# Attention into a squared-ReLU feed-forward: another order for the early columns of L1, weight sets stored from another queue, and earlier norms for two pairs of heads

## The chip, the cores and the metric

The kernel runs on one core of a Trainium2 chip. Its engines have an instruction queue each and run in order: TensorE (PE, matrix products), VectorE (DVE), ScalarE (ACT), GpSimd (POOL) and SyncE (SP, which here only issues DMAs). A queue goes on when the semaphores that its next instruction waits for have come. The metric is the time of one execution on the device in microseconds, as the median of some runs; a profile of one further execution shows each instruction.

## The reference

Two blocks follow one another, in float32; the two weight matrices come as float64.

```python
# q, k, v: (8, 12, 448, 64)
def rmsnorm(x, g):
    rms = np.sqrt(np.mean(x * x, axis=-1, keepdims=True) + 1e-06)
    return x / rms * g
q_n, k_n = (rmsnorm(q, g_q), rmsnorm(k, g_k))
scores = scale * np.matmul(q_n, k_n.transpose(0, 1, 3, 2))
scores = scores - np.max(scores, axis=-1, keepdims=True)
attn = np.exp(scores)
attn = attn / (np.sum(attn, axis=-1, keepdims=True) + 1e-09)
attn_out = np.matmul(attn, v).astype(np.float32)

x = np.ascontiguousarray(attn_out.transpose(0, 2, 1, 3)).reshape(B * S, H * D)   # (3584, 768)
h = x @ w_in            # (3584, 2048)
r = np.maximum(h, 0.0)
g = r * r
return (g @ w_out).astype(np.float32)   # (3584, 768)
```

## The kernel before

**Spans and pairs.** The eight batches are worked on in four spans of two. The twelve heads are taken as six pairs, so a span has twelve pairs of heads: pairs 0 to 11 are span 0, pairs 12 to 23 span 1, and so on. Both large products, L1 (`x @ w_in`) and L2 (`g @ w_out`), are done in the Strassen-Winograd manner: the weights and the activations are split into quadrants, and seven products stand for eight. Of the weights the seven blocks are called A11, S2, S1, S3, A12, A22, S4. The activations' sums are held in `xC` (for L1) and `gC` (for L2) beside `xT` and `gT`, the transposed activations; `combine_x` builds `xC` and `combine` builds `gC`.

**The weights** are prepared once, in span 0, and lie in DRAM as `w1s` and `w2s`. This goes in sets, `n` = 0 to 31 (0 to 15 for `w_in`, 16 to 31 for `w_out`; an even and an odd set make one of 16 groups of seven blocks). The generator `prepare(t)` is a software pipeline cut into four quarters per tick t; `weights(upto)` draws quarters from it until so many have been taken. Counted from the start of tick 0, in tick t stand:

- first quarter: a store of the finished sets (L599, from SP), and DVE clamps the exponents of set t (L604)
- second quarter: ACT converts the low words (L607), DVE shifts bits (L609)
- third quarter: DVE joins the words (L614); POOL makes the totals S3 and S4 of sets t-2 and t-3 (L584), and half a value of set t-1 (L576 on POOL, or, for sets from `MID // 4` on, both halves at once by DVE, L580)
- fourth quarter: ACT takes exponents of set t+1 (L590), POOL the other half value of set t-1 and the totals S1 and S2 (L584), SP loads the words of a later set (L541, L544)

The sets lie in two buffers by turns (`blocks_of`), so a store has to have landed before the second set of blocks after it is written. Three numbers say how far the preparation has come: `EARLY` = 48 quarters by the end of the first stage, `MID` = 86 by the end of the second, `ALL` = 140 in the third.

**The stages of span 0.** They follow one another in program order; the profile's places are in brackets.

1. `attention_alone` (to about 122 us): pairs 0 to 9 (`NAT` = 10), with keys and queries laid out as [112, 4 x ...] per head. Each pair i takes four steps; `norm(i+2)` squares and sums (ACT, DVE), `roots(i+2)` takes the inverse root as Ln and Exp on ACT and one step of refinement on DVE (L730 to L732) and multiplies on POOL (L733). For pairs 10 and 11 the layout is another (`by_squares`: squares of 32 x 32), and `norm(i+2)` at the end of step i calls `squares` (ACT, L740) and `norm_by_squares`: DVE sums, copies and adds (L747 to L752), POOL takes the power -1/2 (L753) and multiplies (L755).
2. The early product with pairs 10 and 11 beside it (122 to 197 us). `first_product(work, 0, 0)` does the blocks A11, S1 and A12 of the first `NE` = 6 of the `HF` = 8 column groups f, three groups of matmuls each, 18 in all (line L1060). `attention(10, 12)` is drawn beside it in 16 pieces, with 38 quarters of the preparation. In it the softmax sums of a pair go out from DVE as `square`, by POOL DMA L1022 to DRAM (`factors`), and come back spread over partitions (L833) into `xT`; DVE multiplies (`finish`, L903), and `combine_x` builds `xC` (L913 to L918, on DVE for pair 11, on POOL for pair 10).
3. `first_product(work, 0)` (197 to 305 us): for f < 6 (`kept`) the other blocks in the order S2, S3, A22, S4, for f = 6 and 7 all seven, 38 groups in all (line L1094). S2 goes into the PSUM tile `pb`, S3 into `pd`, A22 is added onto `pd` once DVE has added `pd` to y and written `g22` (L1112), S4 goes into `pc`. `pb`, `pc` and `pd` take turns in two banks (`bank`, by the counter `turn`). 54 quarters of the preparation are drawn beside it in the first 34 of its 38 steps, and the norms of pairs 12 and 13 (`ahead`).

Then `second_product` of span 0 follows with the attention of span 1 beside it, and so on for the other spans.

**Loads of weight blocks.** `load_blocks(upto)` asks for blocks from `w1s` and `w2s` in the order of their use (`first_uses`, `uses2`), five ahead, into the tile `sw` with five buffers; each is a DMA from SP's queue (L668). It asks only for blocks of sets that count as stored (`written`). SP's queue also carries the loads of q, k and v, the words of the weights, the stores of the sets and the output.

Of the kernel before, what the change touches and what calls it, by code (L numbers as in the profile page):

```python
# [10 lines left out]
F32 = mybir.dt.float32  # L11
U32 = mybir.dt.uint32
AF = mybir.ActivationFunctionType
ALU = mybir.AluOpType
# [373 lines left out]
def attention_then_ffn_bounded(  # L388
# [98 lines left out]
    HW = HC * P  # L487
    WORDS, BLOCKS, EXPS = 7, 2, 4

    EARLY, MID, ALL = 48, 86, 4 * (2 * NFC + 3)  # L490
    assert DM == NW and BLOCKS * 8 * HW + EXPS * NW + 2 * NW <= 3 * HF * S and 2 * NW <= 4 * S and HF % 4 == 0


# [28 lines left out]
    def place_of(n, k):  # L522

        return 7 * int(n >= NFC) if k == A21 else k + int(n < NFC)
# [27 lines left out]
    def prepare(t):  # L552

        def there(n):
            return 0 <= n < 2 * NFC

        def parts(n):
            low, high = pairs_of(words_of(n))  # L560
            return exponents_of(n), exponents_of(n).bitcast(U32), low, high

        def value(n, half):
            if not there(n):
                return

            to = ((A11, A12), (A21, A22)) if n < NFC else ((A11, A21), (A12, A22))
            places = [place_of(n, k) for k in to[n % 2]]
            part = slice(half * HW, (half + 1) * HW)
            if not doubles:  # L570
                nc.gpsimd.tensor_copy(blocks_of(n)[:, places[half]], words_of(n).bitcast(F32)[:, part])
                return
            _, eu, low, _ = parts(n)
            if n < MID // 4:
                dst = blocks_of(n)[:, places[half]]
                nc.gpsimd.tensor_tensor(*[x.bitcast(I32) for x in (dst, low[:, part], eu[:, part])], ALU.add)  # L576
            elif half == 0:
                dst = blocks_of(n)[:, places[0]:places[1] + 1:places[1] - places[0]]
                low, eu = (x.rearrange("p (h m) -> p h m", h=2) for x in (low, eu))
                nc.vector.tensor_tensor(*[x.bitcast(I32) for x in (dst, low, eu)], ALU.add)  # L580

        def total(n, dst, x, y, op):
            if there(n) and n % 2:
                nc.gpsimd.tensor_tensor(*[blocks_of(n)[:, place_of(n, i)] for i in (dst, x, y)], op)  # L584

        def unsigned(n):

            if there(n) and doubles:
                e, _, _, high = parts(n)
                nc.scalar.activation(e, high.bitcast(F32), AF.Abs)  # L590

        if t == 0:
            unsigned(0)
        n = t - 3
        if there(n) and n % 2:
            c = n % NFC // 2
            dst = w1s[c] if n < NFC else w2s[c // 4, :, c % 4]
            first = place_of(n, A11)
            nc.sync.dma_start(dst, blocks_of(n)[:, first:first + 7])  # L599
            written[0] = n + 1  # L600
        if there(t) and doubles:
            e, eu, low, high = parts(t)

            nc.vector.tensor_scalar(e, e, 2.0 ** -15, 1.875 * 2.0 ** 16, ALU.max, ALU.min)  # L604
        yield
        if there(t) and doubles:
            nc.scalar.activation(low.bitcast(I32), low, AF.Copy, scale=2.0 ** -29)  # L607
            bits = banks.get("bits", eu)
            nc.vector.tensor_scalar(bits, eu, 3, 0x3FFFFFF8, ALU.logical_shift_left, ALU.bitwise_and)  # L609
        if t < 3:  # L610
            load_words(t, t - 1)
        yield
        if there(t) and doubles:
            nc.vector.scalar_tensor_tensor(eu, high, 0xC0000000, bits, ALU.bitwise_and, ALU.bitwise_or)  # L614
        total(t - 2, S3, A11, A21, ALU.subtract)
        total(t - 2, S4, A12, S2, ALU.subtract)
        value(t - 1, 0)
        yield
        unsigned(t + 1)
        value(t - 1, 1)  # L620
        total(t - 1, S1, A21, A22, ALU.add)
        total(t - 1, S2, S1, A11, ALU.subtract)
        load_words(t, t - 1)
        yield
# [18 lines left out]
    uses2 = [(m, i) for m in range(HC) for i in (A11, A12)]  # L643
    uses2 += [(m, i) for m in range(HC) for i in (S2, S1, S3, A22, S4)]
    first_uses = [(f, i) for f in range(NE) for i in (A11, S1, A12)]
    first_uses += [(f, i) for f in range(NE) for i in (S2, S3, A22, S4)]
    first_uses += [(f, i) for f in range(NE, HF) for i in range(7)]

    N1 = HF * 7
# [71 lines left out]
    def roots(i):  # L721


        raw, sq = (places_of(qk, i, n)[:SP] for n in range(2))
        rstd = rstds[i]
        flat = rstd.rearrange("p s n -> p (s n)")
        y, t = (small.tile([P, 2 * S // 32], F32, tag=tag, name=tag)[:SP, 0:4 * NJ] for tag in ("half", "other"))
        nc.scalar.activation(y, flat, AF.Ln, scale=2.0 ** -63)
        nc.scalar.activation(y, y, AF.Exp, scale=-0.5, bias=sums["rebias"])
        nc.vector.scalar_tensor_tensor(t, y, -0.5, flat, ALU.mult, ALU.mult)  # L730
        nc.vector.tensor_tensor(t, t, y, ALU.mult)
        nc.vector.scalar_tensor_tensor(flat, t, 1.5, y, ALU.add, ALU.mult)  # L732
        nc.gpsimd.tensor_tensor(sq[:, 0].rearrange("p (j h d) -> p h j d", j=NJ, h=2),  # L733
                                raw[:, 0].rearrange("p (h j d) -> p h j d", j=NJ, h=2),
                                rstd[:, 0].rearrange("p (h j) -> p h j ()", h=2).to_broadcast([SP, 2, NJ, D]),
                                ALU.mult)
# [2 lines left out]
        raw, qkn = (by_squares(i, n).rearrange("p s g e -> p (s g e)") for n in range(2))  # L739
        nc.scalar.activation(qkn, raw, AF.Square)  # L740

    def norm_by_squares(i):
        raw, qkn = (by_squares(i, n) for n in range(2))
        NG = S // 32
        half = small.tile([P, 2 * NG], F32, tag="half", name="half")
        other = small.tile([P, 2 * NG], F32, tag="other", name="other")
        nc.vector.tensor_reduce(half, qkn.rearrange("p s g e -> p (s g) e"), AX, ALU.add)  # L747
        for n in range(4):
            m = n ^ 1
            nc.vector.tensor_copy(other[n * 32:(n + 1) * 32], half[m * 32:(m + 1) * 32])  # L750
        nc.vector.tensor_tensor(half, half, other, ALU.add)
        nc.vector.tensor_scalar(half, half, 1.0 / D, 1e-6, ALU.mult, ALU.add)  # L752
        nc.gpsimd.tensor_tensor(half, half, mhalf, ALU.pow)  # L753
        for s in range(2):
            nc.gpsimd.tensor_tensor(  # L755
                qkn[:, s], raw[:, s],
                half[:, s * NG:(s + 1) * NG].rearrange("p g -> p g ()").to_broadcast([P, NG, 32]), ALU.mult)
        normed[i] = qkn
# [161 lines left out]
    def attention_alone():  # L920


        for i in range(NAT):
            more = i + 1 < NAT
            if 0 < i < NAT - 3:
                load(i + 3)
            scores(i, 0)
            scores(i, 1)
            if i == 0:

                transpose(1, 1, 1)
                scores(0, 2)
                scores(0, 3)
                transpose(1, 0, 0)
                add_up(0, 1)
                norm(2)
                load_v(1)
                values(0, (0, 1))
                load(3)
                yield  # L940
                continue
            if more:
                transpose(i + 1, 1, 0)
            values(i - 1, (2, 3))
            add_up(i, 1)
            if i + 2 < NAT:
                norm(i + 2)
            elif not more:
                load(NAT + 2)
            yield  # L950
            if more:
                transpose(i + 1, 0, 0)
            load_v(i + 1)
            yield
            scores(i, 2)
            scores(i, 3)
            if i + 2 < NAT:
                roots(i + 2)
            total_of(i - 1)
            values(i, (0, 1))  # L960
            finish(i - 1)
            yield
            if added(i) == 3:
                add_up(i, 2)
            combine_x(i - 1)
            if NAT <= i + 3 < NAT + 2:
                load(i + 3)
            if i + 2 >= NAT:
                norm(i + 2)
            yield  # L970
        transposes(NAT)
        values(i, (2, 3))
        total_of(i)
        finish(i)
        combine_x(i)
        if NAT + 2 < 2 * NPAIR:
            squares(NAT + 2)
# [62 lines left out]
    def first_product(work, span, part=1):  # L1040
# [27 lines left out]

        for f in range(HF):
            kept = span == 0 and f < NE  # L1070
            order = (S2, S3, A22, S4) if kept else range(7)
            n = span * (N1 + N2) + f * 7
            if span == 0:
                n = 3 * NE + 4 * f if kept else 7 * f
# [130 lines left out]
    with tc.tile_pool(name="words", bufs=2) as spare["pool"]:  # L1205
# [5 lines left out]
        with tc.tile_pool(name="first", bufs=2, reuse_waits="tile") as work:  # L1211
# [4 lines left out]
            sums["turned"], sums["factors"] = (g[:, 0:S] for g in free[2 * NJ + 2:2 * NJ + 4])  # L1216
            sums["ones"] = work.tile([SP, D], F32, tag="ones", name="ones", bufs=1)
            nc.vector.memset(sums["ones"], 1.0)
            sums["rebias"] = work.tile([SP, 1], F32, tag="rebias", name="rebias", bufs=1)
            nc.vector.memset(sums["rebias"], -31.5 * math.log(2.0))  # L1220
            for u, _ in enumerate(attention_alone()):

# [133 lines left out]
```

## Time and profile before

| | |
|---|---|
| median of 3 runs | 1407.07 us (1401.82 to 1408.52) |
| profiled execution: its time, its span | 1403.64 us, 1401.8 us |
| PE busy | 1344.4 us (96%) |
| DVE, ACT, POOL busy | 851.8, 431.4, 608.1 us |
| SP's queue waiting at L599 for POOL's L584, 0 to 310 us | 52.0 us in 9 waits |
| w1s<-gC and w2s<-gC (stores of sets) | 8 and 8, 1344 KB each, 7.2 and 5.8 us to landing |
| sw<-w1s | 224, 192 KB each, 2.3 us to landing |
| L753, the power of a norm on POOL | 38, 4848 ns each |

How to read it. One execution was profiled. An engine counts as busy while it computes; PE's matmuls are pipelined. The row of slices gives the busy share of 40 equal slices in tenths. A waiting line reads: engine, line, tile that waits <- engine, tile and line that came last, then us in total, number of waits, longest. A line of the timeline reads: start, duration, engine, line, operation, written tile <- read tile, count, and in brackets how long the engine stood idle before and what ended that. "SPq" and "DMA" in it are SP's queue and a transfer. `sw`, `pa` to `pd`, `gT`, `gC`, `xT`, `xC` are the program's tiles; `gC` serves as the staging room of the weights as long as span 0 prepares them.

### The profile page before, as it was taken

The numbers are of one execution on the slowest core, as the hardware profiler recorded it, in microseconds if no ns is written. First come the engines' busy times: TensorE is split into PE (matmuls) and PEld (weight loads), VectorE is DVE, ScalarE is ACT, GpSimd is POOL, SyncE is SP. The second block draws the span as 40 slices with busy tenths as digits, with TensorE's granted clock in tenths as the row PEclk, the third lists the DMA queues.
The fourth block names the chain that finished last, engine by engine and source line by source line (L and its number), as shares of the span: only waits on it lengthen the run. The fifth ranks groups of instructions, "written<-read, shape, count | busy, mean of one in ns | idle before, by whom it ended". The sixth has DMA issues, their size and how long they took to land.

```text
span 1401.8 us, 17013 instructions
## 1 busy us (share of the span) xinstructions
PE 1344.4 (96%) x5646; PEld 641.7 (46%) x5646; DVE 851.8 (61%) x1494; ACT 431.4 (31%) x668; POOL 608.1 (43%) x488
## 2 busy tenths in 40 slices
PE   8997868899999999999999999999999999999998
PEld 3332334444444455544444455554444445555554
DVE  6999857839998633447878723447788743332111
ACT  8884435543333211224333211223333201110000
POOL 6778763526566312445656412355665412221000
PEclk9999999999999999999999999999999999999999
DMA  9786777655667543345566533345656433334443
GB/s 256 209 249 164 272 256 265 182 177 116 126 128 144 120 99 90 85 113 127 125 131 131 128 100 84 90 104 116 133 124 135 107 98 90 85 89 107 106 110 71
DMA packets 428836, 190.66 MB, mean 136 GB/s; under 512 B 290756, under 2 KB 423428, under 8 KB 426692
## 3 DMA queue, kind: packets, MB, share of 16 engines
q1 hardware_dynamic: 421860, 180.39, 50.6%
q0 software_dynamic: 4992, 8.86, 2.4%
q8 instruction: 47, 0.77, 0.2%
q10 hardware_dynamic: 1888, 0.23, 0.1%
q14 instruction: 49, 0.40, 0.1%
HBM read 156.24 MB, written 33.17 MB: 135 GB/s over the span
## 4 chain that ended last, share of the span: by engine, by line
PE 82%; DVE 9%; POOL 3%; DMA 3%; issue 2%; ACT 1%; SPq 0%; POOLq 0%; DVEq 0%; ACTq 0%
PE ps L1163 36%; PE pd L1094 9%; PE pc L1094 9%; PE pa L1094 8%; PE sc L788 7%; PE pav L865 7%; PE pb L1094 4%; DVE gC L614 1%; POOL gC L584 1%; DVE gT L813 1%; DMA sw<-w1s 1%; DMA factors<-square 1%; DVE gC L604 1%; PE sc L796 1%; DVE gC L580 1%
## 5 line engine op out<-in xcount | busy, mean ns | idle before, releaser
L1163 PE MATMUL ps<-gT,sw 128*128 128x448 f32 x752 | 293.0, 543 | 0.0
L1163 PE MATMUL ps<-gC,sw 128*128 128x448 f32 x576 | 225.2, 543 | 0.0
L753 POOL TENSOR_TENSOR half<-half,mhalf 128x28 f32<-128x28 f32 x38 | 184.2, 4848 | 94.5 <-DVE half L752 88.0
L1050 POOL TENSOR_TENSOR gT<-gT 128x448 f32<-128x448 f32 x96 | 94.4, 985 | 289.1 <-ACT gT L1046 289.1
L1163 PEld LDWEIGHTS ps<-gT,sw 128*128 128x128 f32 x752 | 141.2, 190 | 146.3 <-issue 141.6
L1163 PEld LDWEIGHTS ps<-gC,sw 128*128 128x128 f32 x576 | 108.2, 190 | 112.8 <-issue 109.5
L1046 ACT ACTIVATE gT<-gT 128x448 f32<-128x448 f32 x96 | 55.3, 576 | 321.1 <-DVE gT L1112 321.1
L1094 PE MATMUL pa<-xT,sw 128*128 128x448 f32 x312 | 125.8, 540 | 0.0
L788 PE MATMUL sc<-qkT 64*64 64x448 f32 (+1 forms) x1216 | 117.5, 502 | 7.2 <-ACT qkT L765 7.2
L790 ACT ACTIVATE pr<-sc 128x896 f32<-128x896 f32 x89 | 79.3, 915 | 117.9 <-PE sc L788 117.9
L1094 PE MATMUL pb<-xC,sw 128*128 128x448 f32 x192 | 81.1, 561 | 11.9 <-DMA sw<-w1s 10.9
L1094 PE MATMUL pd<-xC,sw 128*128 128x448 f32 x192 | 79.7, 552 | 10.4 <-DVE gT L1112 10.4
L584 POOL TENSOR_TENSOR gC<-gC 128x384 f32<-128x384 f32 x64 | 74.6, 1182 | 34.0 <-DVE gC L580 32.0
L1094 PEld LDWEIGHTS pa<-xT,sw 128*128 128x128 f32 x312 | 59.4, 190 | 57.8 <-issue 57.3
L1112 DVE TENSOR_TENSOR gT<-z,pd 128x448 f32<-128x448 f32 x32 | 19.9, 621 | 106.3 <-PE pd L1094 106.3
L833 POOL DMA_DIRECT2D xT<-factors x76 | 40.1, 532 | 97.8 <-DMA factors<-square 76.2
L755 POOL TENSOR_TENSOR qk<-qk,half 128x448 f32<-128x448 f32 x76 | 80.8, 1083 | 3.0
L1094 PE MATMUL pd<-xT,sw 128*128 128x448 f32 x192 | 77.9, 542 | 0.1
L1094 PE MATMUL pc<-xT,sw 128*128 128x448 f32 x192 | 77.4, 540 | 0.0
L865 PE MATMUL rest<-pr,vt 64*64 64x448 f32 x356 | 74.6, 537 | 0.0
L865 PE MATMUL pav<-pr,vt 64*64 64x448 f32 x356 | 74.6, 537 | 0.0
L788 PEld LDWEIGHTS sc<-qkT 64*64 64x64 f32 x1216 | 42.7, 134 | 57.3 <-issue 40.3
(169 smaller groups left out, 1965.9 us busy)
## 6 DMA issues: line engine op xcount, KB each, us to landing
sw<-w1s SPq DMA_DIRECT2D x224, 192.0 KB, 2.3
sw<-w2s SPq DMA_DIRECT2D x168, 256.0 KB, 3.3
w1s<-gC SPq DMA_DIRECT2D x8, 1344.0 KB, 7.2
w2s<-gC SPq DMA_DIRECT2D x8, 1344.0 KB, 5.8
out_dram<-osb SPq DMA_DIRECT2D x186, 56.0 KB, 1.9
qk<-in_q_dram SPq DMA_DIRECT2D x152, 56.0 KB, 3.6
qk<-in_k_dram SPq DMA_DIRECT2D x152, 56.0 KB, 2.9
xT<-factors POOLq DMA_DIRECT2D x76, 112.0 KB, 3.3
```

The lines of the kernel that those rows point to most:

```text
L584: nc.gpsimd.tensor_tensor(*[blocks_of(n)[:, place_of(n, i)] for i in (dst, x, y)], op)
L753: nc.gpsimd.tensor_tensor(half, half, mhalf, ALU.pow)
L755: nc.gpsimd.tensor_tensor(qkn[:, s], raw[:, s], half[:, s * NG:(s + 1) * NG].rearrange("p g -> p g ()").to_broadcast([P, NG, 32]), ALU.mult)
L788: nc.tensor.matmul(sc[part, h, 0:n], qkT[rows, 0, 1, keys], qkT[rows, 0, 0, of], start=True, stop=True)
L790: nc.scalar.activation(pr, sc[:, :, 0:n], AF.Exp)
L833: nc.gpsimd.dma_start(xT[h * D:(h + 1) * D, b % 2, hp], sums["out"][i % 2].rearrange("(h g) t -> h () (g t)", h=2)[h].to_broadcast([D, S]))
L865: nc.tensor.matmul(into, vs[i][rows, h, c, :], probs[i, c][rows, h, :], start=(c == 0), stop=(c == NF), skip_group_check=True)
L1046: nc.scalar.activation(g, src, AF.Relu)
L1050: nc.gpsimd.tensor_tensor(g, g, g, ALU.mult)
L1094: nc.tensor.matmul(ps, stream[n + at][:, c], rhs[:, c], start=first and c == 0, stop=c == HC - 1, skip_group_check=not first)
L1112: add(g, x, ps, ALU.add)
L1163: nc.tensor.matmul(ps, stream[n][:, c % 4], rhs_of[i][:, c], start=c == 0, stop=c == HF - 1)
```

## The change

- The order of the `kept` columns in span 0's third stage is S2, S3, S4, A22, and the loads follow it; `turn` goes on by one at the start of each such column, so that each column takes four turns of the two banks.
- A pair of sets n-1, n is stored from POOL's queue, in the third quarter of tick n+2 behind its total S4; before, from SP's queue in the first quarter of tick n+3. `written` is set where it was.
- `MID` is 82 for 86: four quarters go from the second stage to the third, and set 20 has its value taken by DVE.
- For pairs 10 and 11 the squares and the sums are made where `roots` stands for the others (third step of pair i), and at the end of the fourth step the inverse root by Ln, Exp and three DVE operations in place of POOL's power; POOL multiplies as before. For that `rebias` has 128 rows, and there are two small tiles more.

```diff
-    EARLY, MID, ALL = 48, 86, 4 * (2 * NFC + 3)
+    EARLY, MID, ALL = 48, 82, 4 * (2 * NFC + 3)
...
-        n = t - 3
-        if there(n) and n % 2:
-            c = n % NFC // 2
-            dst = w1s[c] if n < NFC else w2s[c // 4, :, c % 4]
-            first = place_of(n, A11)
-            nc.sync.dma_start(dst, blocks_of(n)[:, first:first + 7])
-            written[0] = n + 1
+        if there(t - 3) and (t - 3) % 2:
+            written[0] = t - 2
...
         total(t - 2, S3, A11, A21, ALU.subtract)
         total(t - 2, S4, A12, S2, ALU.subtract)
+        n = t - 2
+        if there(n) and n % 2:
+            c = n % NFC // 2
+            dst = w1s[c] if n < NFC else w2s[c // 4, :, c % 4]
+            first = place_of(n, A11)
+            nc.gpsimd.dma_start(dst, blocks_of(n)[:, first:first + 7])
         value(t - 1, 0)
...
-    first_uses += [(f, i) for f in range(NE) for i in (S2, S3, A22, S4)]
+    first_uses += [(f, i) for f in range(NE) for i in (S2, S3, S4, A22)]
...
-        nc.scalar.activation(y, y, AF.Exp, scale=-0.5, bias=sums["rebias"])
+        nc.scalar.activation(y, y, AF.Exp, scale=-0.5, bias=sums["rebias"][:SP])
...
-    def norm_by_squares(i):
+    def norm_by_squares(i, part=None):
...
+        if part == 1:
+            half, y, t = rstds[i], sums["root"], sums["step"]
+            nc.scalar.activation(y, half, AF.Ln, scale=2.0 ** -63)
+            nc.scalar.activation(y, y, AF.Exp, scale=-0.5, bias=sums["rebias"])
+            nc.vector.scalar_tensor_tensor(t, y, -0.5, half, ALU.mult, ALU.mult)
+            nc.vector.tensor_tensor(t, t, y, ALU.mult)
+            nc.vector.scalar_tensor_tensor(half, t, 1.5, y, ALU.add, ALU.mult)
+            return spread_norm(i, half)
...
+        if part == 0:
+            rstds[i] = half
+            return
         nc.gpsimd.tensor_tensor(half, half, mhalf, ALU.pow)
+        spread_norm(i, half)
+
+    def spread_norm(i, half):
+
+        raw, qkn = (by_squares(i, n) for n in range(2))
+        NG = S // 32
         for s in range(2):
             nc.gpsimd.tensor_tensor(
                 qkn[:, s], raw[:, s],
...
             if i + 2 < NAT:
                 roots(i + 2)
+            else:
+                squares(i + 2)
+                norm_by_squares(i + 2, 0)
             total_of(i - 1)
...
             if i + 2 >= NAT:
-                norm(i + 2)
+                norm_by_squares(i + 2, 1)
             yield
...
-            order = (S2, S3, A22, S4) if kept else range(7)
+            order = (S2, S3, S4, A22) if kept else range(7)
+            turn[0] += kept
...
-            sums["rebias"] = work.tile([SP, 1], F32, tag="rebias", name="rebias", bufs=1)
+            sums["rebias"] = work.tile([P, 1], F32, tag="rebias", name="rebias", bufs=1)
+            for name in ("root", "step"):
+                sums[name] = work.tile([P, 2 * S // 32], F32, tag=name, name=name, bufs=1)
```

## The prediction

> **What bounds the kernel now.** I read the row of slices first: from 310 us on TensorE (PE) is busy without a break, so only the first 310 us, span 0 with its attention and its weight preparation, can gain. There I took PE's waits from 122 to 306 us, then asked for the queue behind each.
>
> ```profile
> PE   8997868899999999999999999999999999999998
> ```
>
> ```profile
> PE pb L1094 <- DMA sw<-w1s: 10.9, 2, 7.6
> PE pd L1094 <- DVE gT L1112: 10.4, 6, 2.9
> PE sc L788 <- ACT qkT L765: 7.2, 1, 7.2
> PE pa L1060 <- DMA sw<-w1s: 6.1, 1, 6.1
> PE pc L1060 <- ACT gT L1046: 2.2, 1, 2.2
> PE pa L1060 <- ACT gC L590: 1.5, 1, 1.5
> PE pb L1094 <- DVE gT L1112: 1.0, 1, 1.0
> ```
>
> 17.0 us are waits for weight blocks (sw), 10.4 us are the six A22 groups, 7.2 us the first score of pair 10. SyncE's own waits (0 to 310 us) say why blocks came late:
>
> ```profile
> SPq L599 <- POOL gC L584: 52.0, 9, 10.1
> ...
> SPq L687 <- POOL qk L755: 10.0, 2, 5.9
> ```
>
> A store of a set (L599) waits for GpSimd's last total, and every load behind it in SP's queue waits too. The SP timeline shows both large sw waits starting so:
>
> ```profile
> 159.48 0.34 SPq L599 DMA_DIRECT2D w1s<-gC  x1
> 159.92 1.34 SPq L668 DMA_DIRECT2D sw<-w1s  x2
> ...
> 190.77 0.32 SPq L599 DMA_DIRECT2D w2s<-gC  x1
> 191.19 1.33 SPq L668 DMA_DIRECT2D sw<-w1s  x2
> ```
>
> But behind the second wait (PE idle 189.6 to 197.2) stands another chain, on POOL and DVE: pair 11's softmax factors go out, come back, are spread into xT, and only then can DVE build xC, which the first S2 group reads.
>
> ```profile
> 174.16 0.53 POOL L1022 DMA_DIRECT2D factors<-square  x1
> 181.35 1.05 POOL L833 DMA_DIRECT2D xT<-factors  x2 [6.65 <-DMA factors<-square]
> ```
>
> ```profile
> 185.79 1.14 DVE L903 TENSOR_TENSOR xT<-xC,xT 128x448 f32<-128x448 f32 x1 [9.19 <-DMA xT<-factors]
> ...
> 191.26 1.32 DVE L917 TENSOR_TENSOR xC<-xT,xC 128x448 f32<-128x448 f32 x1
> ```
>
> L917 ends at 192.58, so of that 7.59 us SP's block owns only the last 4.6. The table by stage gives DVE's load while S2 to A22 run:
>
> ```profile
> 197.00:272.00 75.00, 63.45 (x154) 30.29 (x155) 55.60 (x77) 37.86 (x58) 30.87 (x27) 0.95 0.69 241
> ```
>
> The columns are PE 63.45, PEld, DVE 55.60, ACT 37.86, POOL 30.87 of 75 us, clock, DMA share, GB/s.
>
> **What the Trainium skill says.** *DMA: Bandwidth & Descriptors*, "Issuing engines are not separate DMA queues": DMAs issued from any engine run on the same 16 DMA engines; another issuer saves sequencer time only. Here that is the point, as SP's time is what is lost (52 us); bandwidth gains nothing. *SBUF — State Buffer*, "SBUF: two separate sides": a GpSimd-issued DMA has its descriptors written by GpSimd, and a DVE instruction in a two-port mode locks it out; further down, under "A bandwidth-pool intuition that's wrong (but worth ruling out)", it gives about 0.62 us alone and 3.1 us against a DVE copy. This trace has L833 at 0.53 us, 0.52 to 0.55 over 76, so no lockout shows in it. *TensorE: Matmul & The Clock Gate*, "What's actually happening": after an idle window of about 3.4 us PE runs at half clock. Agreed: a group of six takes 2.42 us, but 4.69 after the 6.13 wait, 4.42 after 7.59 and 4.02 after 3.34.
>
> **The change, part by part.**
>
> *Stores to POOL.* 16 stores leave SP. POOL issues them right behind its own total, so it waits for nothing new; `written` advances in the same quarter, so no load is asked for earlier. Cost on POOL: no row shows a 128-row store from POOL. Nearest is L833 with 64 rows, 0.53 us: low end 0.5, high end 3.1 (the skill's price). I take 0.7. Behind a store on POOL wait the values and totals, L733 and the spreads. Landing was 7.2 us from SP and stays about that. SP's queue loses the 52 us, and loads no longer stand behind 1344 KB in the same ring. Pair 10/11's factors share POOL's ring with the stores, but set 13's goes out near 159 and has landed before pair 11's factors at 171; set 15's, which at 173.27 ran into that transfer, now follows it.
>
> *Norms without power.* Two pows of 4.8 us leave POOL. Added: six DVE operations of 0.17 (1.0 us) and four short ACT ones (L728, L729: 0.2 and 0.3). The 7.2 us wait looks like the target, yet DVE is busy 9.75 of 10 us from 110 to 120, and the reductions still precede L764 on DVE, only further ahead. With the copies of L750 taking 0.2 or 0.9 us, the latter beside POOL's tensor work, I put that start at +1.5 us (range -4 to +3). POOL gets ahead and L687's 10 us on SP shrink; nothing at the end reads that directly. Then the 1.5 us wait at 140, a load behind a store, goes: net 0 by group 11 (159.8).
>
> *From group 11 to the first S2.* The load of group 11 has its buffer at 150.7 and lands well before 159.8. 6.13 + 2.27 (cold clock) + 2.19 (pc, ACT held 4.75 us by a POOL that stood waiting) = 10.6 us gone: group 17 ends at 179.0 instead of 189.6. Then xC decides. POOL from 152.4: value 13 twice 2.3, four totals of 13 5.4, store 0.7, value 14 twice 2.3, value 15 2.1, xC of pair 10 4.6, two totals of 15 2.7 = 20 us, so factors at about 172 (it was 174.2: one value and two totals later now by the smaller MID), 3.5 us to land in place of 6.65, spread 1.1, xT 3.5 = 180, L903 1.1, L604 1.3, L916 and L917 2.7: 185. First S2 at 185.0, not 197.2: **gain 12.2**, and the cold start there stays.
>
> *S2, S3, S4, A22.* The six A22 waits (10.4) and their cold 1.8 go only if DVE keeps up: 54.2 us of PE (24 groups at 2.257) plus 2 cold is the floor, before it took 71.0. With MID 82 and set 20's value moved to DVE (0.95), DVE has some 45 quarters, not 43, in this stage. I stepped DVE's order through: z and y 1.3, each of three adds 0.65, L609 + L614 + L580 2.87 and L604 0.57 per tick, 1.7 ticks per column, and 2.05 wherever an L604 follows the ACT chain relu, square, L590 of the same step. It also starts 5 us behind, as L918 and four preparation steps come after L917. S4 of one column gates the next S2, A22 the next S3. Columns then start at 0, 11.6, 22.0, 32.0, 41.8, 57.5 (the norm of pair 12 in it), and the stage ends at 67.7. **Gain 3.3** (15 if DVE's waits vanish, -3 if they grow).
>
> *Last two columns.* The 3.34 wait and 1.6 cold at 287 go; but the S2 of column 6 now waits for the last A22's add, 1.8, and S3 for a z behind pair 13's norm, 2.7. 37.15 becomes 36.5: **gain 0.7**. The last set is stored about 21 us after column 6 starts and lands by 29; its first reader is due at 36, so cover is 4 us after a 3.3 us load.
>
> Sum 12.2 + 3.3 + 0.7 = 16.2. The profiled execution took 1403.64 (span 1401.8 and 1.8 around it): 1387.4. The median, 1407.07, is 3.4 above; from the mean of the three runs, 1405.8, I get **1389**.
>
> **Rivals.** (1) *PE keeps its pace.* The A22 stall was the ping-pong itself; with it gone DVE's 55.6 us of 75 fit and 8 to 12 us more go: 1379. For: L1112 waited 14.6 us for PE in this stage. Against: L604's waits for L590 are in the same window. (2) *Spread stays the bound.* Factors queue in POOL's ring behind a 7.2 us store or the faster stage fills the DMA engines (share 0.72 from 142 to 197, 12 MB then in 42 us, about 300 GB/s), xC is ready at 190, DVE takes the rest back: gain 3 to 9, 1400. For: that transfer took 6.65 beside a store. (3) *Stores hold POOL: slower.* If descriptors wait on DVE's two-port operations and each store costs POOL 3 us or more, five of them in the attention stage stand before L733, where DVE is 97% busy and takes no delay back, one before pair 11's factors, one at the end: seven at 2.3 us extra eat the 16; at 3.3 the kernel is slower by over 0.5%. At 4 extra: 1418. Against: 0.53 us in all 76 rows. (4) *The order does nothing:* if the banks' turn were wrong, S2 would wait where A22 did; the shift by one per column gives each bank a group between, so I keep this in (2).
>
> **How the numbers follow.** My case 0.42 (1383 to 1396), (1) 0.22, (2) 0.21, (3) 0.15. Within 0.5% is 1399 to 1413, about what this measurement can tell from no change. Faster: 0.42 + 0.22 + 0.09 of (2) = 0.73; same: 0.12 of (2) + 0.02 of (3) = 0.14; slower 0.13. The range 1374 to 1402 leaves out most of (3), a piece of (2) and the top of (1).
>
> **What would show it.** Right: SP's waits for L584 at stores gone; w1s and w2s issued from POOL at under 1 us; PE's L1060 wait for sw gone; first S2 near 185, its wait put down to L917 or L903, not sw; pd's waits for L1112 small with DVE nearly full in that stage; the 7.2 us before pair 10's scores still there. Wrong: a POOL store of several us; DVE idle on L580 until w2s has landed; ps at the second product waiting for sw<-w2s; or that 7.2 us gone, which would mean DVE had room I deny.

## The result, and the profile after

The changed kernel takes 1393.69 us (median; 1391.37 to 1395.48), 0.9913 of the kernel before, 95% interval 0.989 to 0.9936. The forecast was 1389 (1374 to 1402): the sign and the range hold, the point is 4.7 us low. In the profiled execution (1395.48 us, span 1393.5) the gap is larger: 8.1 us over the 1387.4 that the sum gave.

In the kernel after, the lines that matter have other numbers: clamp, shift and join of the weights' words on DVE are L599, L604, L609 (before L604, L609, L614), the store is L617, the totals stay L584 and the values L576, the matmuls of the stage with S2 to A22 are L1118 (L1094), its `z` L1125 and its added blocks L1136 (L1112), the attention's DVE sums L833 (L813), `xT` L923 (L903) and `xC` L936 to L938 (L916 to L918). The row of slices has the same shape; what is won lies in the first 310 us again:

```profile
PE   8987979799999999999999999999999999999997
```

PE's waits of the kernel after in its first 310 us (engine, tile, line <- what came last: us, times, longest):

```profile
PE pt L791 <- ACT qkT L793: 7.2, 4, 3.1
PE pc L1118 <- DVE z L1125: 5.4, 2, 4.6
PE pb L1118 <- DVE gT L1136: 4.4, 2, 3.2
PE pb L1118 <- ACT gT L1086: 3.8, 1, 3.8
PE tot L899 <- DVE gT L833: 3.3, 2, 3.1
PE sc L816 <- ACT gT L820: 3.0, 1, 3.0
PE tot L899 <- DVE gT L912: 2.7, 1, 2.7
PE pd L1118 <- DVE gT L1136: 2.7, 3, 1.5
```

The 17.0 us for `sw` are gone, the A22 waits fell from 10.4 to at most 2.7 us (the last line). What is left from the first S2 on waits for DVE, but for 3.8 us for ACT's copy L1086; ahead of it the transposes `pt` of the attention wait 7.2 us for ACT, 3.8 in the kernel before. SP's queue, same stretch, has no wait of a store any more, but it still waits for POOL elsewhere, at the loads of q and k (L316) longer than before (22.4 us in 4 waits there):

```profile
SPq L316 <- POOL qk L734: 37.2, 5, 11.1
...
SPq L544 <- POOL gC L576: 8.3, 2, 8.0
SPq L688 <- POOL qk L775: 8.0, 3, 4.2
...
SPq L669 <- DMA w2s<-gC: 5.0, 1, 5.0
```

Where the forecast's 8 us went is seen in the marks of the path (us from the start of the span):

| mark | before | forecast | after |
|---|---|---|---|
| first score of pair 10 | 122.68 | 124 | 129.77 |
| group 11 of the early product | 165.95 | 159.8 | 165.10 |
| `xC` complete (L917; after L937) | 192.58 | 185.0 | 190.74 |
| first S2 | 197.21 | 185.0 | 187.88 |
| column 6 | 268.25 | 252.7 | 260.72 |
| end of L1 | 305.40 | 289.2 | 296.39 |

A caution for all marks of this document: two executions don't start alike. The clamp ahead of the first store begins at 40.99 us in the kernel before and at 42.10 in the kernel after; in the runs below it begins at 41.15 to 43.23, and at 43.15 in `o_only`, which changes only what comes long behind it. So I take 1.1 us of the differences between before and after in this table as there from the start.

The rest of the delay is there before the early product starts, and DVE is late at each mark. In DVE's timeline of the kernel after there are eight instructions of 2.46 to 5.05 us in the first 330 us, where the longest of the kernel before takes 1.91. Seven stand behind stores, one, at 153 us, behind the POOL DMAs that spread a pair's factors (L853). One of them, with POOL beside it:

```profile
98.91 0.59 POOL L617 DMA_DIRECT2D w1s<-gC  x1 [0.30 <-POOL gC L584]
99.53 3.92 POOL L576 TENSOR_TENSOR gC<-gT,gC 128x384 int32<-128x384 int32 x4
```

```profile
99.35 5.05 DVE L833 TENSOR_TENSOR gT<-gT 112x896 f32<-112x896 f32 x1
104.33 0.61 DVE L933 TENSOR_TENSOR xC<-xT 128x448 f32<-128x448 f32 x1
```

The same work in the kernel before:

```profile
96.09 8.56 POOL L576 TENSOR_TENSOR gC<-gT,gC 128x384 int32<-128x384 int32 x4
```

```profile
96.87 1.91 DVE L813 TENSOR_TENSOR gT<-gT 112x896 f32<-112x896 f32 x1
98.70 0.61 DVE L913 TENSOR_TENSOR xC<-xT 128x448 f32<-128x448 f32 x1
...
99.71 1.90 DVE L813 TENSOR_TENSOR gT<-gT 112x896 f32<-112x896 f32 x1
```

Before, POOL and DVE take turns: four values need 8.56 us, and DVE goes on between them. After, right behind the store, POOL runs its four values back to back (0.98 us each), and DVE's L833, which by the trace began just ahead of the first, ends only after the last: 5.05 us instead of 1.9. DVE's busy time grows from 851.8 to 861.3 us; some 2 us of that are new work (six operations of 0.17 us for the norms, one value of 0.95), by the prediction's prices. The Trainium skill, *SBUF — State Buffer*, "Who interferes with whom", has the ground for it: DVE and GpSimd share one port pair under an exclusive lock, a DVE instruction with two SBUF inputs, as L833 is, collides there, and "issue order, not op shape, decides who blocks". The trace agrees on the collision. On the order it doesn't decide: DVE's start, 99.35, lies ahead of POOL's first value (99.53) but behind POOL's store (98.91), and it then stood for four POOL instructions, not one. I call this a hold.

### The profile page after: what moved, and what is told of

It reads as the page before. It is cut to its first block, busy times and chain, and to the rows that moved or that the text cites. A ratio compares the mean times of both kernels' runs of the same rounds, so it can differ in the third digit from the quotient of the medians.

```text
span 1393.5 us, 17025 instructions
## 1 busy us (share of the span) xinstructions
PE 1346.0 (97%) x5646; PEld 641.6 (46%) x5646; DVE 861.3 (62%) x1501; ACT 432.4 (31%) x672; POOL 599.1 (43%) x500
## 4 chain that ended last, share of the span: by engine, by line
PE 84%; DVE 8%; ACT 2%; issue 2%; DMA 2%; POOL 1%; SPq 0%; ACTq 0%; DVEq 0%
PE ps L1187 36%; PE pd L1118 8%; PE pc L1118 8%; PE pa L1118 8%; PE sc L808 8%; PE pav L885 7%; PE pb L1118 4%; DVE gC L599 1%; PE sc L816 1%; DVE gC L609 1%; PE pa L1083 1%; DVE gC L580 1%; DMA gT<-in_moe_w_in_dram 1%; DVE gT L833 1%; PE tot L899 1%
## 5 line engine op out<-in xcount | busy, mean ns | idle before, releaser
L767 POOL TENSOR_TENSOR half<-half,mhalf 128x28 f32<-128x28 f32 x36 | 174.3, 4842 | 79.3 <-DVE half L763 76.0
L1118 PE MATMUL pa<-xT,sw 128*128 128x448 f32 x312 | 125.7, 539 | 0.0
L584 POOL TENSOR_TENSOR gC<-gC 128x384 f32<-128x384 f32 x64 | 77.6, 1229 | 27.6 <-DVE gC L580 25.5
L1118 PE MATMUL pb<-xC,sw 128*128 128x448 f32 x192 | 81.2, 561 | 8.4 <-DVE gT L1136 4.4
L775 POOL TENSOR_TENSOR qk<-qk,half 128x448 f32<-128x448 f32 x76 | 82.6, 1107 | 14.5 <-DVE half L754 7.2
L1118 PEld LDWEIGHTS pa<-xT,sw 128*128 128x128 f32 x312 | 59.3, 190 | 58.0 <-issue 57.4
L1118 PE MATMUL pc<-xT,sw 128*128 128x448 f32 x192 | 79.4, 550 | 5.4 <-DVE z L1125 5.4
L1136 DVE TENSOR_TENSOR gT<-z,pd 128x448 f32<-128x448 f32 x32 | 19.8, 620 | 99.2 <-PE pd L1118 99.2
L853 POOL DMA_DIRECT2D xT<-factors x76 | 40.0, 531 | 95.5 <-DMA factors<-square 61.6
L1118 PE MATMUL pd<-xT,sw 128*128 128x448 f32 x192 | 78.1, 543 | 3.0 <-DVE z L1125 2.2
L1118 PE MATMUL pd<-xC,sw 128*128 128x448 f32 x192 | 77.6, 540 | 1.9 <-DVE gT L1136 1.9
```

The costliest lines, as they stand in the source:

```text
L775: nc.gpsimd.tensor_tensor(qkn[:, s], raw[:, s], half[:, s * NG:(s + 1) * NG].rearrange("p g -> p g ()").to_broadcast([P, NG, 32]), ALU.mult)
L853: nc.gpsimd.dma_start(xT[h * D:(h + 1) * D, b % 2, hp], sums["out"][i % 2].rearrange("(h g) t -> h () (g t)", h=2)[h].to_broadcast([D, S]))
L1118: nc.tensor.matmul(ps, stream[n + at][:, c], rhs[:, c], start=first and c == 0, stop=c == HC - 1, skip_group_check=not first)
L1136: add(g, x, ps, ALU.add)
```

## The experiments

Each ratio is against the kernel before on the same chip. "Holds" are DVE instructions over 2.4 us in the first 330 us.

**Three parts, each alone.** The smaller `MID` has no run of its own. `s_only` is the kernel before with this hunk (and the old store taken out):

```diff
+        n = t - 2
+        if there(n) and n % 2:
...
+            nc.gpsimd.dma_start(dst, blocks_of(n)[:, first:first + 7])
```

> The kernel before, with the stores alone moved to POOL (third quarter of tick n+2); order of columns, norms and MID as before. Theory A (a store on POOL frees SP, but the POOL instructions behind it then hold DVE off the shared port): DVE instructions of 3 to 5 us stand beside most stores in the first 200 us, pair 10's first score starts 4 to 6 us later than before (122.7), and still the sw waits of PE in the second stage are gone; 6 to 10 us faster than before. Theory N (the later start of pair 10's scores comes from the moved norms): that start stays within 2 us of 122.7, no DVE instruction over 2.5 us beside a store, and 13 to 18 us faster than before.

1402.37 us, 0.9973 (0.9963 to 0.9982): 3.8 us, less than the 6 to 10 of theory A and the 13 to 18 of theory N. The waits for `sw` are gone and seven holds are there, the first three where the kernel after has them (2.94 us at 43, 4.55 at 65, 5.05 at 99); pair 10's score comes at 128.89, and the first S2 at 198.47, no sooner than before. PE's waits of `s_only`:

```profile
PE pd L1095 <- DVE gT L1113: 12.5, 6, 3.3
PE pc L1061 <- ACT gT L1047: 10.5, 1, 10.5
...
PE sc L789 <- ACT qkT L766: 5.5, 1, 5.5
```

So the block on SP was real, and the time behind it went to waits for DVE and ACT.

`o_only` is the order, with the loads following it, and the turn of the banks:

```diff
-            order = (S2, S3, A22, S4) if kept else range(7)
+            order = (S2, S3, S4, A22) if kept else range(7)
+            turn[0] += kept
```

> The kernel before, with S2, S3, S4, A22 and the turn of the banks alone. If DVE sets the pace there, as the prediction had it: the six waits of PE for A22 (10.4 us) go, waits for z and for other adds come, the stage from first S2 to column 6 takes 67 to 71 us (before 71.0), 0 to 4 us faster in all. If PE keeps its pace: that stage takes 58 to 62 us, and 8 to 12 us faster.

1400.42 us, 0.9959 (0.9945 to 0.9973): 5.8 us, between the two. The stage took 62.9 us by PE's marks, near the second theory's 58 to 62 and 10 less than in the kernel after. The difference is where it starts: here the first S2 still waits 7.9 us for `sw`, until 200.29, and meanwhile DVE works off the preparation that otherwise stands before `z`. Counted from the end of `xC` (194.23) the stage is 69.0 us long, against 70.0 in the kernel after. So a wait taken from PE takes DVE's time for catching up with it. One DVE instruction takes 2.47 us here, at 155, behind POOL's DMAs of the factors (2.44 at 153 in `n_only`): short holds come without the new stores too.

`n_only` is the norms of pairs 10 and 11 without the rest:

```diff
+            else:
+                squares(i + 2)
+                norm_by_squares(i + 2, 0)
...
-                norm(i + 2)
+                norm_by_squares(i + 2, 1)
```

> The kernel before, with the norms of pairs 10 and 11 alone changed. Theory A: pair 10's first score starts within 2.5 us of 122.7, and the time is within 3 us of before. Theory N: it starts 5 to 7 us later, and the kernel is 3 to 7 us slower. If the norm's power was the cost that the change meant to save: it starts 3 us or more earlier, and the kernel is faster by as much.

1405.29 us, 0.9997 (0.9987 to 1.0007): nothing. Pair 10's score comes at 125.99, 3.3 us late, not 7, and 1.1 of them are there at 42 us, ahead of all norms of this part. That lies between the two theories' marks; as an account of the whole delay, the norms fall.

**Is it the DMA or its load?** `b_tiny` leaves the stores on SP and adds 16 writes of one float per partition from POOL at the places of the new stores:

```diff
         total(t - 2, S4, A12, S2, ALU.subtract)
+        n = t - 2
+        if there(n) and n % 2:
+            nc.gpsimd.dma_start(tiny[n // 2], blocks_of(n)[:, place_of(n, S4), 0:1])
```

> The kernel before, its stores still on SP, with one further DMA of one float per partition from POOL behind each total S4 of an odd set (16 of them, into a scratch tensor). Theory A: DVE instructions of 3 to 5 us stand beside these as beside the real stores, pair 10's first score starts 3 to 6 us later, and the kernel is 3 to 10 us slower. If it is the real store's bytes or the missing wait of SP that matter: DVE as before, and within 2 us of before.

The holds are there again, same instructions, same lengths (2.93, 4.54 and 5.04 us at 42, 64 and 98): they come with a DMA issued by POOL at this place, not with the 1344 KB. But the time is 1439.95 us, 1.0245 (1.0227 to 1.0264), which neither theory had, and which holds don't explain: PE waits 46.5 us for `sw` from 0 to 340 us, as the loads of `sw` land after 9.3 us instead of 5.5 (median, first 310 us).

`b_const` takes the source from a constant that nothing writes, so that the DMA does not stand 0.3 us for POOL's own total:

```diff
+            nc.gpsimd.dma_start(tiny[n // 2], pad)
```

> The kernel before, with 16 small DMAs from GpSimd (one float in each partition) at the places of the new stores, as in b_tiny, but from a constant that nothing writes, so that the DMA does not stand 0.3 us for GpSimd's own total. Theory W, that short wait for its own total is what sets off the long holds: none of DVE's instructions of 3 to 5 us at 42, 64 and 98 us, at most two over 2.4 us in all, and the time within 4 us of the kernel before. Theory P2, any DMA issued ahead of additions of GpSimd does it: the same holds at 42, 64 and 98 us as in b_tiny. If b_tiny's 34 us come from the small writes themselves, they come again here (1435 to 1445).

1444.66 us, 1.0265 (1.0244 to 1.0286): the small writes cost it again. Of the three early holds two are gone; at 100 us POOL and DVE take turns again behind the DMA:

```profile
100.42 0.59 POOL L623 DMA_DIRECT2D tiny<-pad  x1
101.03 6.35 POOL L580 TENSOR_TENSOR gC<-gT,gC 128x384 int32<-128x384 int32 x3
```

The one at 44 us stays (2.54), and three more of 4.44 to 4.61 us stand elsewhere, each beside values that run back to back behind such a DMA. So the short wait of a store for its own total isn't needed for a hold.

**Where the store stands.** Four versions of the kernel after. `a_pad` puts a small write of POOL between the store and the values:

```diff
             nc.gpsimd.dma_start(dst, blocks_of(n)[:, first:first + 7])
+            nc.gpsimd.memset(pad, 0.0)
```

> The kernel after, with one small write on GpSimd (one float in each partition) behind each store, so that the first instruction behind GpSimd's DMA is no longer an addition of 128x384. Theory P1, the run of back-to-back GpSimd additions that holds DVE off is set off by the DMA right ahead of it, and any other instruction in between ends it: of the eight DVE instructions over 2.4 us at most three are left, the first S2 comes 3 us sooner or more, and the time is 4 to 10 us under that of the kernel after (1384 to 1390). Theory P2, what matters is that the DMA has set GpSimd and DVE out of step, or that GpSimd has a backlog: the same DVE instructions stand for the same 3 to 5 us, and the time is within 3 us of the kernel after.

1393.22 us, 0.991 (0.9896 to 0.9924), with six holds, 5.09 us at 99 among them. An instruction in between doesn't break it.

`a_late` issues the store at the start of the next tick, where SP did it before. There two values of POOL stand ahead of it and two behind, instead of four behind (the text on record has totals behind it; by the trace two values come first):

```diff
+        n = t - 3
+        if there(n) and n % 2:
...
+            nc.gpsimd.dma_start(dst, blocks_of(n)[:, first:first + 7])
```

> The kernel after, with each store issued from GpSimd where SyncE issued it before, at the start of the tick three behind its set, and so ahead of totals L584 of the next set but one instead of ahead of values L576. Theory P2 (a run of back-to-back additions follows a GpSimd DMA wherever it stands): 6 to 9 DVE instructions over 2.4 us again, at other places, and the time within 4 us of the kernel after. Theory P3 (it needs values L576 right behind, which have no wait of their own): at most three are left, and the time is 3 to 8 us under the kernel after, unless the later landing of a set lets loads wait for it (a wait of SyncE for w1s<-gC or w2s<-gC of over 3 us would show that).

1391.57 us, 0.9899 (0.9883 to 0.9915): the holds go but for one of 2.69 us, which begins ahead of a store; pair 10's score comes at 125.42 and the first S2 at 182.78, 5.1 us before that of the kernel after. Column 6 begins at 254.32, 6.4 us before. But its second group waits, and L1 ends at 294.90, only 1.5 us before that of the kernel after. PE from 254 us, and DVE's wait behind it (190 to 265 us), in `a_late`:

```profile
254.32 2.42 PE L1117 MATMUL pa<-xT,sw 128*128 128x448 f32 x6
262.94 4.72 PE L1117 MATMUL pb<-xC,sw 128*128 128x448 f32 x6 [6.21 <-DVE gT L1135]
```

```profile
DVE gC L580 <- DMA w2s<-gC: 4.6, 1, 4.6
```

A value waits for its buffer until 258.29, as the store from there, half a tick later in the program than in the kernel after, went out only at 252.01, behind a norm's power (L766) on POOL's queue; the kernel after sent it at 240.69. That is the price of the delay, which the prediction had listed as a sign of being wrong.

`a_mixed` keeps that place for `w1s` only and gives the stores of `w2s` their own back:

```diff
+        n = t - 3
+        if there(n) and n % 2 and n < NFC:
...
+        n = t - 2
+        if there(n) and n % 2 and n >= NFC:
```

> The kernel after, with the stores of w1s at a_late's place and those of w2s at their own. If a_late's gain up to the first S2 (182.8 instead of 187.9 us) was only lost again in DVE's 4.6 us wait for w2s<-gC: that wait is gone, the first S2 comes at 183, column 6 at 257 to 259 and the time is 1386 to 1390. If DVE gives the gain back in another way: column 6 at 260 or later, and the time within 2 us of a_late's 1391.6.

1391.04 us, 0.9895 (0.9876 to 0.9914). The wait for `w2s` is gone, and L1 ends at 292.24, 2.7 us before that of `a_late`; the median is that of `a_late`. Column 6 comes at 256.50. The marks on record for it decide nothing: they rest on 262.9 for `a_late`, which is the second group; its column 6 starts at 254.32. A hold stands in these columns, behind the first store of `w2s`. DVE in `a_mixed`:

```profile
188.57 4.49 DVE L605 TENSOR_SCALAR gC<-gC 128x768 f32<-128x768 f32 x1
```

`a_behind` issues each store behind the first two values, a quarter later than the kernel after and a quarter earlier than `a_late`:

```diff
         value(t - 1, 1)
+        n = t - 2
+        if there(n) and n % 2:
...
+            nc.gpsimd.dma_start(dst, blocks_of(n)[:, first:first + 7])
```

> The kernel after, with each store on GpSimd issued behind the two values L576 that follow its last total, some 2 to 4 us later than in the kernel after, and earlier than in a_late. While the values are GpSimd's own, the store then has nothing to wait for. Theory W (the wait of a store for GpSimd's own total sets off the holds): at most three DVE instructions over 2.4 us before 190 us, first S2 3 to 5 us sooner, no wait for w2s<-gC of over 3 us as a_late had, time 3 to 7 us under the kernel after (1387 to 1391). Theory P2: six or more of them at other places, time within 3 us of the kernel after.

1388.75 us, 0.9885 (0.9867 to 0.9902), the best of all; its interval overlaps that of the kernel after, so that it is faster than that one rests on the trace as well. One instruction is over 2.4 us (2.76, begun ahead of a store), and DVE does not wait for `w2s`. POOL and DVE at the places of the two holds shown above:

```profile
96.04 4.57 POOL L576 TENSOR_TENSOR gC<-gT,gC 128x384 int32<-128x384 int32 x2
100.56 0.59 POOL L621 DMA_DIRECT2D w1s<-gC  x1
101.18 3.42 POOL L576 TENSOR_TENSOR gC<-gT,gC 128x384 int32<-128x384 int32 x2
```

```profile
99.66 1.91 DVE L833 TENSOR_TENSOR gT<-gT 112x896 f32<-112x896 f32 x1
...
188.82 1.36 DVE L599 TENSOR_SCALAR gC<-gC 128x768 f32<-128x768 f32 x1
```

The clamp that took 4.49 us in `a_mixed` takes 1.36 here, 3.13 less. Column 6 comes at 253.37 instead of 256.50, and L1 ends at 289.67 instead of 292.24. In this pair of executions a hold in this stretch goes to PE nearly in full: DVE is on the path.

The traces also show a pattern in when a hold comes. In the kernel after, each of the eight held instructions begins while POOL is issuing a DMA, or as the issue ends, 0.15 to 0.61 us after that DMA's start. In `a_behind`, at the stores of 66, 101 and 160 us, DVE's instruction had begun 0.8 to 0.9 us ahead of the store; it took 1.66 to 1.91 us, and POOL's values took up to 1.7 us each. In `b_const`, too, DVE's instruction had begun 0.8 us ahead of the DMA at 65 and 100 us, where holds went. There are exceptions (at 79.8 us of the kernel after a clamp begins 0.58 us after the store's start and takes 0.55; at 77.8 us of `b_const` a held one began 0.9 us ahead of the DMA), and no run set DVE's start alone. So this is where to look, not a cause shown.

**Does DVE pace S2 to A22?** `a_poolvalue` gives POOL all values, 12 additions fewer for DVE and 24 more for POOL:

```diff
-            if n < MID // 4:
+            if n < 2 * NFC:
```

> The kernel after, with the values of sets 20 to 31 on GpSimd too (24 additions of 128x384 at 0.98 us) instead of 12 of 0.95 us on DVE. The step on trial: from the first S2 to the last A22 the columns are bound by DVE's work. If they are: 8 or so of the 12 lie in that stage, it goes from 72.8 us to about 65, and the time falls 5 to 8 us. If they are bound by GpSimd holding DVE off (the rival): 16 more additions of GpSimd in the stage take at least as much from DVE as they give, the stage stays within 2 us or grows, and the time is the same or up to 10 us longer.

1393.81 us, 0.9918 (0.9904 to 0.9933), like the kernel after. Its stage beside that of the kernel after (PE, PEld, DVE, ACT, POOL busy, clock, DMA share, GB/s):

```profile
185.81:260.01 74.20, 64.04 (x145) 30.31 (x146) 59.83 (x72) 35.58 (x55) 56.85 (x52) 0.86 0.74 257
```

```profile
187.88:260.72 72.84, 61.44 (x145) 28.74 (x146) 62.15 (x81) 34.61 (x53) 40.82 (x36) 0.93 0.74 262
```

This is the rival's outcome. Nine DVE instructions fewer, at 0.95 us, are 8.6 us of work; DVE's busy time falls by 2.3. Most of the rest came back beside POOL's 16 more additions: ten clamps (L599) take 10.4 us in all for 7.7, six sums `y` (L1128) 7.3 for 4.4. DVE also stood idle for longer, 14.4 us for 10.7. So work moved from DVE to POOL does not unload DVE. That DVE paces the stage rests on PE's waits and on the pair above, not on this run.

**The norms within the whole.** `a_oldnorm` is the kernel after without the third part:

```diff
-            else:
-                squares(i + 2)
-                norm_by_squares(i + 2, 0)
...
-                norm_by_squares(i + 2, 1)
+                norm(i + 2)
```

> The kernel after, with the norms of pairs 12 and 13 as before (with the power on GpSimd, later). Theory N0, from the run of the norms alone (0.9997 of the time before): they give nothing here either, the time is within 2 us of the kernel after. Theory N1, they pay only beside the stores and the order, since there GpSimd holds stores as well and two powers of 4.8 us come ahead of what the first S2 or the A22 of column 5 needs: 4 to 8 us longer than the kernel after.

1396.9 us, 0.9934 (0.992 to 0.9948): some 3 us longer than the kernel after, between the two theories, and the two intervals overlap. (The pairs whose norms it sets back are 10 and 11; the text on record has 12 and 13.) In the traces the difference is smaller: its first S2 begins at 188.45 for 187.88 and waits once more for `xC`, until 191.35, column 6 begins at 261.46 for 260.72, and L1 ends at 298.81 for 296.39; of these 2.4 us 1.0 were there at 42 us (the clamp begins at 43.11 for 42.10). So the norms may pay a little beside the other parts, while alone they pay nothing; why, these runs don't show. Stores and order alone, 0.27% and 0.41%, make about this kernel's 0.66%, the smaller `MID` included; with the norms it is 0.87%.

## Why the prediction was right, and where it was off

*Stores to POOL.* Price and landing as forecast: 0.56 to 0.64 us on POOL for 0.7, 7.2 us median to landing (5.2 to 10.5), SP's 52 us of store waits gone, loads of `sw` landing after 3.7 instead of 5.5 us (median, first 310 us; 4.6 in `s_only`). Missing from the sum was the term on the other side: what DVE loses behind such a DMA. Rival (3) asked for this collision, but in one direction, DVE stopping POOL's descriptors; it ran the other way. I took DVE's durations beside POOL from a trace in which the two take turns, and gave them no range.

*Norms.* Pair 10's score moved by 7.1 us, outside -4 to +3 around 1.5; 1.1 of it were there at 42 us. In `a_behind`, which has the same norms and no holds up to there, it moved by 2.2 (124.86), 0.5 of it there at 42 us, and in `n_only` by 3.3, of which 1.1. So the norms' term is 1.7 to 2.2 us, close to the forecast, and some 4.3 us are the missing one. I also priced the new ACT operations by their length alone. Ln stood 7.51 us at the head of ACT's queue for DVE's L763, with pair 9's work on the scores (L820) behind it, and PE got a wait of 3.0 us that I had not named (4.5 in `n_only`). The 7.2 us wait did not stay as one but as 3.0, 2.0, 2.7 and 3.1.

*Group 11.* No wait before it, as said; it is 5.3 us late with all before it. `a_behind` has it at 159.29 for 159.8.

*To the first S2.* Gain 9.3 for 12.2. The chain was the one named, factors, spread, L923, clamp, L936, L937, and it ended 5.7 us late: 3.2 as the spread came late (factors out at 174.9 for 172, landing 4.3 for 3.5), 3.1 as the clamp L599 took 4.37 us for 1.3 behind a store, less 0.5 for a faster L923. In `a_behind` L937 ends at 184.63 for 185.0. One thing was drawn wrongly: PE does not wait for L937 to start the group. Its start waited 3.85 us for ACT's copy L1086, which I had not named; it came 2.9 us before the end of L937, and the group took 4.14 us. So the stage by PE's marks begins sooner and is longer by as much.

*S2 to A22.* DVE paces it, as forecast: from 96 to 265 us it waited 0.6 us for PE, though 8.6 for ACT's L590, which the forecast had in it, and 3.6 for the squares of the norms. By PE's marks the stage took 72.8 us for 67.7, a loss of 1.8 instead of a gain of 3.3; from the end of L937 it is 70.0, and 68.7 in `a_behind`. The steps 10.1, 9.5, 9.8, 15.2, 10.8 of the later columns are the forecast's 10.4, 10.0, 9.8, 15.7, 10.2. The first column failed: 14.5 from the end of L937 (14.9 in `a_behind`) for 11.6. Five DVE instructions stand ahead of `z`, 6.8 us in `a_behind` where I had 5, and a join of 1.75 between `y` and the first L1136.

*Last two columns.* 35.7 for 36.5, with the two waits that were named (2.2 on `z`); the second product did not wait for `w2s`.

*The sum.* Column 6 came 8.0 us later than forecast, and in `a_behind`, which has no hold behind a store, 0.7 later. Of the 7.3 us between the two 0.6 were there at 42 us; some 6.7 are the missing term in this pair of executions. The median of `a_behind`, 1388.75, is the forecast's 1389; that of the kernel after is 4.9 above it (3.9 by the two ratios). That `a_behind` meets the marks so closely is in part luck: its first column took 3.3 us more than forecast, the five behind it 2.3 less. And 1405.8 less 16.2 is 1389.6, which I wrote as 1389.

Of the rivals, (1) fails with DVE's load, and its 62.9 us stage appears only in `o_only`, where DVE had a PE wait to catch up in. The 14.6 us that spoke for it are those from 197 to 309 us; up to 272 us, in the stage itself, L1112 waited 6.8 us for `pd`. (2) is right that DVE takes part of the gain back, but the spread took 4.3 us, not 6.65, and was not the bound.

## What to carry to other kernels

When a wait is taken from the engine at the end of a chain, ask which other engine used that wait to catch up, and count from that engine's mark. Before a DMA is put on GpSimd's queue, look at what stands behind it there: with DVE the pacing engine, as here, not ahead of a run of GpSimd additions, but between them, and not so late that its buffer is waited for. Before marks of two traces are compared, look at one that lies ahead of the change. And a new operation is priced by its wait at the head of its queue, not by its length.

## What the hardware showed that I had not expected

- A DMA of GpSimd costs 0.6 us of issue there and can cost some 3 us on DVE (4.54 us at 65 us for a clamp that takes 1.37 at the same place before): the additions behind it can run back to back (3.92 us for four, against 8.56 when taking turns), and a DVE instruction stands until the last is done. What decides between the two ways stays open; in these traces it goes with whether DVE's instruction begins ahead of the DMA or during its issue.
- Sixteen writes of 0.5 KB, four bytes in each row, from GpSimd's queue made the whole kernel 33 to 39 us slower. Each took 12.2 to 12.5 us to land; the first 310 us moved 205 to 208 GB/s instead of 227, while the packets of the main queue took 88.8 to 91.8% of the 16 engines' time instead of 72.9. Whether it is the small rows or the queue that slows the others was not separated; the 16 stores of 1344 KB from the same queue did not do it.
